# Block attention and a token mixer on one core: loading in float32 from the sync queue and casting on GpSimd, in place of casting in the GpSimd queue's transfers

## The chip, the core and the metric

The kernel runs on one core of a Trainium2 chip. A core has five engines that run side by side: TensorE (PE; its weight loads are listed apart as PEld), VectorE (DVE), ScalarE (ACT), GpSimd (POOL) and SyncE (SP). SP only issues transfers here; POOL issues transfers and can also compute. Sixteen DMA engines move the data between HBM and the on-chip memory SBUF. The metric is the device time of one execution in microseconds (us); less is better.

## What is computed

The inputs are q, k and v in float32, each 8 batches x 8 heads x 576 positions x 64, and three weights. First comes attention inside chunks of 64 positions (nine chunks a head), then a token mixer over the joined heads:

```python
scores = scale * np.matmul(q_c, k_c.transpose(0, 1, 2, 4, 3))   # per chunk of 64
attn = np.exp(scores); attn = attn / np.sum(attn, axis=-1, keepdims=True)
out = np.matmul(attn, v_c)
x = out.transpose(0, 2, 1, 3).reshape(B, S, H * D)              # 8 x 576 x 512
wq = x @ w_q; wk = x @ w_k                                       # 512 -> 64
W_tok = scale * np.einsum('bsd,btd->bst', wq, wk)
mixed = np.einsum('bst,btd->bsd', W_tok, x)
y = np.maximum(mixed, 0.0) @ w_out                              # 8 x 576 x 512, float32
```

## The kernel before, in words

The work is ordered by hand over batches; no scheduler moves anything, and each engine runs its instructions in the order of the text. Step n of the main loop runs the attention of batch n (`Attn`) woven with the mixer of batch n - 1 (`Mix`), and between them up to three pieces of the output product of an earlier batch (`fill`, `out_unit`). Step 8 has only the last mixer, and after it the remaining output pieces are flushed.

The attention of one batch has three groups g of q and k. `transposes(g)` (L150) turns q and k on PE into PSUM, and VectorE copies the result to SBUF (L156). `scores(g)` (L166) multiplies, ScalarE takes the exponential (L174). `av(hl)` (L193) multiplies with v, whose last column of ones also gives the row sums; VectorE takes the reciprocal (L201) and scales into `x_nat` (L202). The mixer transposes `x_nat` (`xt_part`, L226, copied by L233 and L235), projects it (`wqk`, L242), turns that (`wkn`, L254, copies L258 and L259), forms a 64 x 512 product (`gram`, L264) and applies it with the ReLU (`mixed`, L276 and L283). `out_unit` (L294) multiplies with w_out, ScalarE copies to `osb` (L302), and SP stores `osb` in four transfers (L307).

Loads are issued two batches ahead, by `load(b)`: `load_qk` (L100) and `load_v` (L113). All go out on POOL's queue, with float32 in HBM and float16 in SBUF, so the cast happens in the transfer. A q or k piece is 128 float32 (two rows of 64) for each partition and group, a v piece is one row of 64. For batch 0 q and k come in three parts each, for the others in one part for each half of the heads. SP issues only the stores.

The tile `in` of q and k has three buffers, as has v (`v_bufs`), so a load waits until the batch three before it has been used. `osb` has four buffers. PSUM is one pool of four buffers of two banks, shared by all products in turn. In `in` the half of the heads (hg) lies outside of the positions, so each transpose takes 64 columns for one hg and writes to 64 partitions: 24 of them in a group.

Of the kernel before, what the change touches and what calls it, by code (L numbers as in the profile page):

```python
# [9 lines left out]
F16 = mybir.dt.float16  # L10
F32 = mybir.dt.float32
# [5 lines left out]
def kernel(  # L17
# [15 lines left out]
    nc = tc.nc  # L33
    B, H, S, D = q.shape
    DM = moe_w_out.shape[0]
    DH = moe_w_q.shape[1]
    P = 128
    CH = 64
    NCH = S // CH
    NHG = 2  # L40
    NX = (H // NHG) * NCH
    NG = 3
    XG = NX // NG
    UG = XG // 4
# [6 lines left out]
    ts, ds = bass.ts, bass.ds  # L51

    const = ctx.enter_context(tc.tile_pool(name="const", bufs=1))
    in_pool = ctx.enter_context(tc.tile_pool(name="inp", bufs=3))
    qk_pool = ctx.enter_context(tc.tile_pool(name="qkp", bufs=2))
    e_pool = ctx.enter_context(tc.tile_pool(name="ep", bufs=2))
    rec_pool = ctx.enter_context(tc.tile_pool(name="rec", bufs=4))
# [7 lines left out]
    def psum(name, shape, dt=F32):  # L65
        return ps_pool.tile(shape, dt, name=name, tag="ps")

    ident = const.tile([P, P], F16, name="ident")
# [4 lines left out]
    NVB = 3  # L73
    v_bufs = [const.tile([P, NX, VP], F16, name=f"v{i}") for i in range(NVB)]
# [6 lines left out]
    for t in g_bufs:  # L81
# [3 lines left out]
    qr = [  # L85
        t.rearrange("b h s d -> b (h s d)")
        for t in (q, k)
    ]

    def load_qk(b):  # L90
        tiles = [
            in_pool.tile([P, NHG, NG * UG, P], F16, name=f"in{ti}", tag=f"in{ti}")
            for ti in range(2)
        ]
        parts = [ts(g, UG) for g in range(NG)] if b == 0 else [slice(0, NG * UG)]
        for part in parts:
            for ti in range(2):
                src = qr[ti][b].rearrange("(g u p e) -> g p u e", g=NHG, p=P, e=P)
                for hg in range(NHG):
                    nc.gpsimd.dma_start(  # L100
                        tiles[ti][:, hg, part, :], src[hg][:, part, :]
                    )
        return tiles

    def load_v(b):
        vt = v_bufs[b % NVB]
        src = v[b].rearrange("(g h) s d -> g (h s) d", g=NHG)
        src = src.rearrange("g (y o p r) d -> g o r p y d", o=2, p=32, r=2)
        dst = vt.rearrange("p (y o) d -> p o y d", o=2)
        for o in range(2):  # L110
            for half in range(2):
                for r in range(2):
                    nc.gpsimd.dma_start(  # L113
                        dst[ds(half * CH + r * 32, 32), o, :, 0:D],
                        src[(half + o) % 2, o, r],
                    )
        return vt

    wqk16 = const.tile([P, NDC, 2 * DH], F16, name="wqk16")
# [2 lines left out]
    def load_weights():  # L122
        nc.gpsimd.dma_start(
            wqk16[:, :, 0:DH], moe_w_q.rearrange("(i p) j -> p i j", p=P)
        )
        nc.gpsimd.dma_start(
            wqk16[:, :, DH:], moe_w_k.rearrange("(i p) j -> p i j", p=P)
        )
        nc.gpsimd.dma_start(wout16[:], moe_w_out.rearrange("(i p) m -> p i m", p=P))


    class Attn:
# [8 lines left out]
        def transposes(self, g):  # L141
            tp = psum("tp", [P, 2, 1024], F16)
            for ti in range(2):
                cols = tp[:, ti, 0 : UG * 2 * P].rearrange(
                    "p (u x r c) -> p u r x c", u=UG, r=2, x=4
                )
                for u in range(UG):
                    for r in range(2):
                        for hg in range(NHG):
                            nc.tensor.transpose(  # L150
                                cols[ds(hg * D, D), u, r],
                                self.qk_in[ti][:, hg, g * UG + u, ds(r * D, D)],
                                ident[:],
                            )
            sb = qk_pool.tile([P, 2, UG * 2 * P], F16, name="qk", tag=f"qk{g}")
            nc.vector.tensor_copy(sb[:], tp[:, :, 0 : UG * 2 * P])  # L156
            self.qk[g] = sb
# [131 lines left out]
    def out_unit(bp, rmx, t0, nt):  # L289

        op = psum("op", [P, 2, 512])
        for t in range(nt):
            for i in range(NDC):
                nc.tensor.matmul(  # L294
                    op[:, t, :],
                    lhsT=rmx[:, i, ts(t0 + t, P)],
                    rhs=wout16[:, i, :],
                    start=(i == 0),
                    stop=(i == NDC - 1),
                )  # L300
        osb = osb_pool.tile([P, 2, DM], F32, name="osb", tag="osb")
        nc.scalar.copy(osb[:, 0:nt, :], op[:, 0:nt, :])  # L302
        rows = out_rows[ds(2 * S * bp + P * t0, P * nt), :]
        rows = rows.rearrange("(t c p r) m -> c r p t m", c=2, r=2, p=32)
        for c in range(2):
            for r in range(2):
                nc.sync.dma_start(  # L307
                    rows[c, r], osb[ds(c * CH + r * 32, 32), 0:nt, :]
                )

    inputs = {}

    def load(b):
        inputs[b] = (load_qk(b), load_v(b))

    ctx.enter_context(tc.manual_schedule())

    load(0)
    load_weights()
    load(1)  # L320

    att, mix, outs = None, None, []

    def fill(n=1):
        for _ in range(n):
            if outs:
                outs.pop(0)()

    for n in range(B + 1):
        if n + 2 < B:  # L330
            load(n + 2)
        att = Attn(n) if n < B else None
        if att:
            att.transposes(0)
            att.transposes(1)
        if mix:
            mix.xt_part(0)
        if att:
            att.transposes(2)
        fill()  # L340
        if mix:
            mix.xt_part(1)
        if att:
            att.scores(0)
            att.scores(1)
        if mix:
            mix.wqk()
        fill()
        if att:
            att.scores(2)  # L350
            att.av(0)
            att.av(1)
        if mix:
            mix.wkn()
        fill()
        if mix:
            mix.gram()
        if att:
            att.av(2)
            att.av(3)  # L360
        if mix:
            for i in range(NDC):
                mix.mixed(i)
            bp, rmx = mix.b // 2, mix.rmx
            tiles = ((0, 2), (2, 2)) if mix.b % 2 == 0 else ((4, 2), (6, 2), (8, 1))
            outs += [
                lambda t0=t0, nt=nt, bp=bp, rmx=rmx: out_unit(bp, rmx, t0, nt)
                for t0, nt in tiles
            ]
        mix = Mix(n, att.x) if att else None  # L370
# [31 lines left out]
```

The softmax here doesn't subtract the row's maximum and nothing guards it: scores larger than these inputs give would overflow.

## Time and profile before

| what | value |
|---|---|
| time, median of 2 runs | 163.25 us (163.04 to 163.47) |
| the profiled execution's own time | 163.47 us |
| its span, from first to last instruction | 161.7 us |
| PE busy | 118.5 us (73%) |
| DVE, ACT busy | 64.9 us, 73.3 us |
| POOL busy (nearly all of it issuing transfers) | 82.1 us (51%) |
| read from HBM, written to HBM | 29.62 MB, 9.44 MB |
| loads of q and k of batches 1 to 7 | 288 KB each as written, 28 transfers |
| loads of v | 72 KB each as written, 64 transfers |
| stores | 128 KB x64 and 64 KB x16, 4.0 and 3.8 us from issue to landing |

How to read it: in a group of the profile stand the line, the engine, the operation, the tiles written and read, the count, then the busy time and the mean of one; after the bar the idle time just ahead of it and what ended it. In a timeline a row is the start, the busy time, the engine and line, with the idle time before it in brackets. "The stretches" are a view of chosen windows with the busy time of each engine (PE, PEld, DVE, ACT, POOL), then the clock granted to PE, the mean number of packets in work on each DMA engine, and GB/s written.

### The profile page before, as it was taken

The numbers are of one execution on the slowest core, as the hardware profiler recorded it, in microseconds if no ns is written. First come the engines' busy times: TensorE is split into PE (matmuls) and PEld (weight loads), VectorE is DVE, ScalarE is ACT, GpSimd is POOL, SyncE is SP. The second block draws the span as 40 slices with busy tenths as digits, with TensorE's granted clock in tenths as the row PEclk, the third lists the DMA queues.
The fourth block names the chain that finished last, engine by engine and source line by source line (L and its number), as shares of the span: only waits on it lengthen the run. The fifth ranks groups of instructions, "written<-read, shape, count | busy, mean of one in ns | idle before, by whom it ended". The sixth has DMA issues, their size and how long they took to land. (4 is left out here: it accounts for less than half of the span.)

```text
span 161.7 us, 5174 instructions
## 1 busy us (share of the span) xinstructions
PE 118.5 (73%) x2304; PEld 72.1 (45%) x2304; DVE 64.9 (40%) x119; ACT 73.3 (45%) x101; POOL 82.1 (51%) x113
## 2 busy tenths in 40 slices
PE   0567302494999589978994998789948997886840
PEld 0345201473475347635653565346535653442310
DVE  2032180166462556164616461646165516411000
ACT  3002300045366454756374637563747374844640
POOL 7999994597399397479349735961100000000000
PEclk9999999999599999999999699999999999999998
DMA  2999999999999999999999999999980044335165
GB/s 25 117 129 126 89 183 180 160 143 173 141 85 178 198 257 184 174 243 210 214 165 230 235 177 180 159 183 237 171 202 12 4 130 102 97 82 155 29 177 147
DMA packets 82886, 24.59 MB, mean 152 GB/s; under 512 B 77744, under 2 KB 78256, under 8 KB 82864
## 3 DMA queue, kind: packets, MB, share of 16 engines
q0 software_dynamic: 76976, 14.82, 110.9%
q1 hardware_dynamic: 5888, 9.44, 20.0%
q8 instruction: 18, 0.29, 0.7%
q14 instruction: 4, 0.03, 0.0%
HBM read 29.62 MB, written 9.44 MB: 242 GB/s over the span
## 5 line engine op out<-in xcount | busy, mean ns | idle before, releaser
L156 DVE COPY qk<-tp 128x1536 f16<-128x1536 f16 x24 | 22.4, 955 | 27.3 <-PE tp L150 27.3
L302 ACT COPY osb<-op 128x1024 f32<-128x1024 f32 (+1 forms) x20 | 18.4, 927 | 22.9 <-PE op L294 16.7
L202 DVE TENSOR_TENSOR x_nat<-xp,rec 128x640 f16<-128x640 f32 x32 | 26.4, 825 | 1.1
L174 ACT ACTIVATE est<-sp 128x768 f16<-128x768 f32 x24 | 18.7, 814 | 13.9 <-PE sp L166 13.9
L113 POOL DMA_DIRECT2D v_88<-in_v_dram x24 | 16.0, 685 | 14.5 <-DMA in_1885<-in_k_dram 5.0
L201 DVE RECIPROCAL rec<-xp 128x10 f32<-128x10 f32 x32 | 6.9, 215 | 38.0 <-PE xp L193 38.0
L113 POOL DMA_DIRECT2D v_87<-in_v_dram x24 | 15.9, 682 | 8.3 <-DMA in_1514<-in_k_dram 3.2
L233 ACT COPY xt<-tx 128x1152 f16<-128x1152 f16 x8 | 9.0, 1122 | 23.8 <-PE tx L226 23.8
L294 PE MATMUL op<-wout_104,rmx_102 128*128 128x512 f16 x72 | 17.4, 380 | 0.7 <-ACT rmx_102 L283 0.5
L294 PE MATMUL op<-wout_104,rmx_101 128*128 128x512 f16 x72 | 17.2, 379 | 0.5 <-ACT est L174 0.5
L264 PE MATMUL gp<-x_nat,wn 128*128 128x512 f16 x40 | 11.1, 412 | 7.9 <-DVE wn L259 7.9
L113 POOL DMA_DIRECT2D v_89<-in_v_dram x16 | 10.6, 687 | 8.5 <-DMA in_1131<-in_q_dram 2.7
L226 PE MATMUL tx<-ident,x_nat 128*128 128x128 f16 x160 | 12.1, 225 | 0.1
L226 PEld LDWEIGHTS <-x_nat 128*128 128x128 f16 x160 | 10.0, 101 | 2.8 <-issue 0.2
L235 DVE COPY xt<-tx 128x1152 f16<-128x1152 f16 x8 | 6.1, 756 | 11.6 <-PE tx L226 11.6
L193 PEld LDWEIGHTS <-est 64*64 64x64 f16 x640 | 7.6, 118 | 6.7 <-issue 3.8
L294 PEld LDWEIGHTS <-rmx_102 128*128 128x128 f16 x72 | 6.5, 98 | 8.5 <-ACT rmx_102 L283 1.9
L283 ACT ACTIVATE rmx_102<-mp 128x576 f16<-128x576 f32 x16 | 9.1, 656 | 2.3 <-PE mp L276 2.3
L283 ACT ACTIVATE rmx_101<-mp 128x576 f16<-128x576 f32 x16 | 9.1, 656 | 2.3 <-PE mp L276 2.3
L242 PE MATMUL wp<-xt,wqk_103 128*128 128x512 f16 (+1 forms) x64 | 9.5, 285 | 0.7 <-DVE xt L235 0.4
L294 PEld LDWEIGHTS <-rmx_101 128*128 128x128 f16 x72 | 6.4, 98 | 7.3 <-issue 0.8
L264 PEld LDWEIGHTS <-wn 128*128 128x128 f16 x40 | 3.4, 100 | 13.2 <-DVE wn L259 10.2
(85 smaller groups left out, 163.5 us busy)
## 6 DMA issues: line engine op xcount, KB each, us to landing
out_dram<-osb SPq DMA_DIRECT2D x64, 128.0 KB, 4.0
v_87<-in_v_dram POOLq DMA_DIRECT2D x24, 72.0 KB, 7.2
v_88<-in_v_dram POOLq DMA_DIRECT2D x24, 72.0 KB, 8.3
v_89<-in_v_dram POOLq DMA_DIRECT2D x16, 72.0 KB, 7.9
out_dram<-osb SPq DMA_DIRECT2D x16, 64.0 KB, 3.8
in_107<-in_q_dram POOLq DMA_DIRECT2D x6, 96.0 KB, 3.3
in_108<-in_k_dram POOLq DMA_DIRECT2D x6, 96.0 KB, 3.3
in_132<-in_q_dram POOLq DMA_DIRECT2D x2, 288.0 KB, 7.6
```

Of the source, the lines that this page charges most:

```text
L113: nc.gpsimd.dma_start(dst[ds(half * CH + r * 32, 32), o, :, 0:D], src[(half + o) % 2, o, r],)
L156: nc.vector.tensor_copy(sb[:], tp[:, :, 0 : UG * 2 * P])
L174: nc.scalar.activation(e.rearrange("p o y c -> p o (y c)"), sp[:, :, 0 : XG // 2 * CH], AF.Exp, scale=scale_attn,)
L193: nc.tensor.matmul(xs[o0 : o0 + CH, hg, j, 0 : D + 1], lhsT=self.e[g][r0 : r0 + CH, xl % 2, xl // 2, :], rhs=self.v[r0 : r0 + CH, x, 0 : D ...
L202: nc.vector.tensor_tensor(out=self.x.rearrange("p j (g h d) -> p g j h d", g=NHG, h=HH)[:, :, :, hl, :], in0=xs[:, :, :, 0:D], in1=rec[:, ...
L226: nc.tensor.transpose(tx[:, i2, ts(j, P)], self.x[:, j, ts(2 * half + i2, P)], ident[:],)
L233: nc.scalar.copy(xt[:], tx[:, :, 0:S])
L242: nc.tensor.matmul(wp[:, ds(c0, n)], lhsT=wqk16[:, i, :], rhs=self.xt[i // 2][:, i % 2, ds(c0, n)], start=(i == 0), stop=(i == NDC - 1),)
L264: nc.tensor.matmul(gp[:, 0:DM], lhsT=self.wn[:, j].rearrange("p t d -> p (t d)"), rhs=self.x[:, j, :], start=(j == 0), stop=(j == NJ - 1),)
L283: nc.scalar.activation(self.rmx[:, i, ds(self.col0, S)], mp[:, 0:S], AF.Relu, scale=scale_moe)
L294: nc.tensor.matmul(op[:, t, :], lhsT=rmx[:, i, ts(t0 + t, P)], rhs=wout16[:, i, :], start=(i == 0), stop=(i == NDC - 1),)
L302: nc.scalar.copy(osb[:, 0:nt, :], op[:, 0:nt, :])
```

## The change

The loads move to SP's queue and stay float32, into new tiles `raw0`, `raw1` and `rawv` with two buffers each. GpSimd then casts to float16: `cast_qk` makes six tiles a batch (q and k of each of the three groups, 768 elements for each partition) and `cast_v` one (2,304 elements). The casts of batch n + 1 are issued at the start of step n, after the loads of batch n + 2; the casts of batch 0 come before the loads of the weights, which stay on POOL. While it casts, `cast_qk` puts hg inside of the positions, so a transpose takes all 128 columns and both hg at once: 12 in a group. The stores stay on SP, in one order with the loads. In a step, the loads of batch n + 2 come before the step's stores.

```diff
+    raw_pool = ctx.enter_context(tc.tile_pool(name="rawp", bufs=2))
...
     def load_qk(b):
-        tiles = [
-            in_pool.tile([P, NHG, NG * UG, P], F16, name=f"in{ti}", tag=f"in{ti}")
+        src = [t[b].rearrange("(g u p e) -> g p u e", g=NHG, p=P, e=P) for t in qr]
+        raw = [
+            raw_pool.tile([P, NHG, NG * UG, P], F32, name=f"raw{ti}", tag=f"raw{ti}")
             for ti in range(2)
         ]
         parts = [ts(g, UG) for g in range(NG)] if b == 0 else [slice(0, NG * UG)]
         for part in parts:
             for ti in range(2):
-                src = qr[ti][b].rearrange("(g u p e) -> g p u e", g=NHG, p=P, e=P)
                 for hg in range(NHG):
-                    nc.gpsimd.dma_start(
-                        tiles[ti][:, hg, part, :], src[hg][:, part, :]
-                    )
-        return tiles
+                    nc.sync.dma_start(raw[ti][:, hg, part, :], src[ti][hg][:, part, :])
+        return raw
+
+    def cast_qk(raw, g):
+        pair = []
+        for ti in range(2):
+            t = in_pool.tile(
+                [P, UG, 2, NHG, D], F16, name=f"in{ti}{g}", tag=f"in{ti}{g}"
+            )
+            nc.gpsimd.tensor_copy(
+                t[:],
+                raw[ti][:, :, ts(g, UG), :].rearrange("p g u (r d) -> p u r g d", r=2),
+            )
+            pair.append(t)
+        return pair
 
     def load_v(b):
-        vt = v_bufs[b % NVB]
+        raw = raw_pool.tile([P, NX, D], F32, name="rawv", tag="rawv")
...
-                    nc.gpsimd.dma_start(
-                        dst[ds(half * CH + r * 32, 32), o, :, 0:D],
+                    nc.sync.dma_start(
+                        dst[ds(half * CH + r * 32, 32), o],
                         src[(half + o) % 2, o, r],
                     )
+        return raw
+
+    def cast_v(b, raw):
+        vt = v_bufs[b % NVB]
+        nc.gpsimd.tensor_copy(vt[:, :, 0:D], raw[:])
         return vt
...
                 for u in range(UG):
                     for r in range(2):
-                        for hg in range(NHG):
-                            nc.tensor.transpose(
-                                cols[ds(hg * D, D), u, r],
-                                self.qk_in[ti][:, hg, g * UG + u, ds(r * D, D)],
-                                ident[:],
-                            )
+                        nc.tensor.transpose(
+                            cols[:, u, r],
+                            self.qk_in[g][ti][:, u, r].rearrange("p g d -> p (g d)"),
+                            ident[:],
+                        )
...
     def load(b):
-        inputs[b] = (load_qk(b), load_v(b))
+        raws[b] = (load_qk(b), load_v(b))
+
+    def cast(b):
+        rqk, rv = raws.pop(b)
+        inputs[b] = ([cast_qk(rqk, g) for g in range(NG)], cast_v(b, rv))
...
     load(0)
+    cast(0)
     load_weights()
     load(1)
...
         if n + 2 < B:
             load(n + 2)
+        if n + 1 < B:
+            cast(n + 1)
```

More of the change, by code (lines that the diff above doesn't have):

```diff
@@ L97, in load_qk @@
             for ti in range(2):
-                src = qr[ti][b].rearrange("(g u p e) -> g p u e", g=NHG, p=P, e=P)
                 for hg in range(NHG):
-                    nc.gpsimd.dma_start(
-                        tiles[ti][:, hg, part, :], src[hg][:, part, :]
-                    )
-        return tiles
+                    nc.sync.dma_start(raw[ti][:, hg, part, :], src[ti][hg][:, part, :])
[12 more added lines that the diff above has]
+        return pair
     def load_v(b):
-        vt = v_bufs[b % NVB]
+        raw = raw_pool.tile([P, NX, D], F32, name="rawv", tag="rawv")
         src = v[b].rearrange("(g h) s d -> g (h s) d", g=NHG)
         src = src.rearrange("g (y o p r) d -> g o r p y d", o=2, p=32, r=2)
-        dst = vt.rearrange("p (y o) d -> p o y d", o=2)
+        dst = raw.rearrange("p (y o) d -> p o y d", o=2)
         for o in range(2):
@@ L311 @@
     inputs = {}
+    raws = {}
     def load(b):
-        inputs[b] = (load_qk(b), load_v(b))
+        raws[b] = (load_qk(b), load_v(b))
+    def cast(b):
+        rqk, rv = raws.pop(b)
+        inputs[b] = ([cast_qk(rqk, g) for g in range(NG)], cast_v(b, rv))
     ctx.enter_context(tc.manual_schedule())
     load(0)
+    cast(0)
     load_weights()
```

## The prediction

> **What bounds the kernel now.** I read the slices of the page first, then the tensor engine in order of time, then the list of waits, then the stretches.
>
> ```profile
> PE   0567302494999589978994998789948997886840
> DMA  2999999999999999999999999999980044335165
> PEclk9999999999599999999999699999999999999998
> ```
>
> One slice is 161.7 / 40 = 4.04 us. The DMA row is full from slice 1 to slice 28, that is to about 118 us, and PE is near full from slice 9 on. So two things look busy, and the order of time has to say which one sets the end.
>
> ```profile
> 19.12 1.31 PE L193 MATMUL xp<-v_87,est 64*64 64x65 f16 x78 [2.78 <-DMA v_87<-in_v_dram]
> ...
> 25.40 0.32 PE L150 MATMUL tp<-ident,in_132 128*64 128x128 f16 x1 [4.97 <-DMA in_132<-in_q_dram]
> 27.37 0.85 PE L150 MATMUL tp<-ident,in_132 128*64 128x128 f16 x11 [1.66 <-DMA in_132<-in_q_dram]
> 29.00 0.32 PE L150 MATMUL tp<-ident,in_133 128*64 128x128 f16 x1 [0.78 <-DMA in_133<-in_k_dram]
> 30.65 0.85 PE L150 MATMUL tp<-ident,in_133 128*64 128x128 f16 x11 [1.34 <-DMA in_133<-in_k_dram]
> ...
> 37.36 0.53 PE L193 MATMUL xp<-v_88,est 64*64 64x65 f16 x40
> ...
> 44.87 0.53 PE L150 MATMUL tp<-ident,in_146 128*64 128x128 f16 x12
> ...
> 60.43 0.53 PE L150 MATMUL tp<-ident,in_419 128*64 128x128 f16 x12
> ...
> 124.06 0.53 PE L150 MATMUL tp<-ident,in_1884 128*64 128x128 f16 x12
> ...
> 139.66 0.72 PE L226 MATMUL tx<-ident,x_nat 128*128 128x128 f16 x10
> ```
>
> The bracket names what ended the idle time. Up to batch 1 (in_132, in_133) every long bracket names a load. From batch 2 (44.87) on none does: batch 3 starts at 60.43, batch 7 at 124.06, the drain at 139.66. That is 94.8 us for six batches, 15.8 each (a clean one 15.6, one at a lower clock 16.3). The reader sees two regimes: 44.9 us of filling bound by loads, then 116.8 us (161.7 less 44.9) in which PE's own order is the limit.
>
> ```profile
> PE tp L150 <- DMA in_107<-in_q_dram: 6.7, 6, 4.3
> PE tp L150 <- DMA in_132<-in_q_dram: 6.6, 2, 5.0
> PE xp L193 <- DMA v_87<-in_v_dram: 2.8, 1, 2.8
> PE tp L150 <- DMA in_133<-in_k_dram: 2.1, 2, 1.3
> ```
>
> The list of waits agrees: the columns are total, times, longest, and only batches 0 and 1 appear. Last, two stretches in which nearly only one kind of load ran (q/k, then v):
>
> ```profile
> 26.50:29.00 2.50, 0.85 (x11) 0.60 (x12) 0.00 (x0) 0.00 (x0) 0.66 (x1) 1.00 1.83 182
> 29.60:32.00 2.40, 1.35 (x26) 1.35 (x28) 0.46 (x1) 0.00 (x0) 1.41 (x3) 1.00 2.37 153
> ```
>
> The last column is GB/s written as f16, so what is read as f32 is twice that: 364 and 306 GB/s. A batch has 2.36 MB of f32 q and k and 1.18 MB of v: 6.5 + 3.9 = 10.3 us. Yet the q loads of batches 2 to 7 follow each other by 12 to 15 us (31.54, 44.69, 56.80, 70.45, 84.54, 99.68 on POOL), because POOL's last v issues of each batch wait for earlier landings. A load stream that always has work could so be up to 3 us a batch faster than it is.
>
> **What the Trainium skill says.** "DMA: Bandwidth & Descriptors", SWDGE vs HWDGE vs iDMA: a cast in flight is possible from the GpSimd queue alone, and descriptors there are computed by GpSimd. The trace agrees on the second half: L113 is 64 issues of 0.66 to 0.74 us busy time on POOL. The same page, Issuing engines are not separate DMA queues: whoever issues, the same 16 engines do the work. So the move to SP gives no bandwidth of its own. "GPSIMD Engine Reference", 3.1: a one-input loop costs 1.03 to 1.8 cycles an element at 1.2 GHz, so an estimate of 0.66 to 1.15 us for 768 elements; no cast is in this trace, but two nearby rows are (below). "SBUF — State Buffer", Who interferes with whom: a VectorE instruction with at most one SBUF input outside the two-port modes does not block GpSimd. Here L156, L201, L202 and L235 all read PSUM (L202 with one small SBUF input), so I charge no contention; no run here shows it yet.
>
> **The change part by part.**
>
> Transposes. Before, 72 half transposes a batch: 44.87 to 46.34 for 48 and 47.00 to 47.79 for 24 give 2.26 us, 31 ns each, as two halves of the array run beside each other. After, 36 full ones. The nearest row is L226, ten full transposes from 46.34 to 47.00, 66 ns each: 36 x 66 = 2.37 us. Halving the count saves nothing; it costs 0.1 us a batch, 0.7 us over the six PE-bound ones. Bounds: 56 ns (two halves at the quickest pace, 12 in 0.33 us) to 73 ns (L226's busy time by ten), so -0.2 to +0.4 a batch.
>
> Issue. POOL loses 40 issues of q/k (0.76 to 1.04 us) and 64 of v (0.69), about 80 of its 82.1 us. SP gains these 104; its 80 stores took 0.43 us each (median), so 12 x 0.43 = 5.2 us a batch beside 10 stores' 4.3: under 15.6, hidden. In the start it matters: POOL needed until 16.07 us to issue batch 0; SP needs 20 x 0.43 = 8.6, and the stream fills.
>
> Casts. Six of 768 and one of 2304 elements a batch on POOL. A one-element memset took 99 ns, one of 128 elements 204 ns, a select over 128 elements 304 ns: 0.82 to 1.60 ns an element. So 0.73 to 1.33 us for a q or k cast, 1.99 to 3.79 for v; I take the middle, 1.03 and 2.9. A batch is 9.1 us (6.4 to 11.8), under 15.6, so hidden from batch 2 on. The casts run a batch or more ahead of PE: `in` and `v` have three buffers, and their waits on PE are for a batch three back. What is queued behind a waiting cast is the next cast, and at the start the three weight loads, needed only by L242 at 36 us.
>
> Loads. Same descriptors, f32 written instead of f16. I take the read rates above, 10.3 us a batch. The trace has no load without a cast. Bounds: below, 9.1 (an assumed 12% for the cast in flight, no row shows it); above, time going with bytes read plus written, x 1.33, 13.7 us.
>
> The filling, step by step. First landing: before, issue 1.29 to landing 4.30; SP starts at about 0.8, so q/k of batch 0 land by 2.8 + 6.5 = 9.3 and v by 13.2. v's cast ends at 16.1, where before v landed at 19.1. Then POOL issues the weights, 2.3 us. Batch 1's q and k land at 13.2 + 6.5 = 19.7; the weights' 1.6 MB share the engines, some 2.5 us, so 22.2, and v at 26. The casts then set the pace: k's first at 23.3, third at 27.5, v at 30.4. So the L193 of batch 1 starts at 30.5 instead of 37.36: 6.9 us earlier. If casts are at their upper bound, it is 32.7; at the lower, it is about 29.5, since PE's own order after k's landing then binds. Gain of the fill 4.7 to 7.9.
>
> After it, batch 2 starts at 44.9 - 6.9 = 38.0. With v of batch 1 at 26 and 10.3 a batch, k of batch 2 lands near 32.5, cast by 38, just in time; k of batch 3 near 43, with need at 53.6: hidden.
>
> Stores. They now stand behind loads in SP's order. The stores of batch 0's rows, ready near 44, wait until the load of batch 4 is issued, and that waits for batch 2's casts and for the eight loads before it. That load ends near 57, so they land near 60. Osb has four buffers, five units in two batches, so the fifth copy at about 60 can just be held: I charge 1.5 us once (0 to 5). The end is untouched: no loads stand before the last stores.
>
> Sum: 161.7 - 6.9 + 0.7 + 1.5 = 157.0 us of span; the profiled execution took 163.47, 1.8 more than its span, so 158.8. That execution is 0.2 over the median 163.25, so the forecast beside the median is 158.5 us, 2.9% faster.
>
> **Rivals.**
>
> *The gain is eaten.* The fill shortens by 3 us only, and L302's copies wait several times for osb. For it: the stores' late landing above, and ACT's copies already head PE's L254 waits (3.1 us). Against it: SP catches up once loads run ahead. 161.7 - 3 + 0.7 + 4, with 1.8 less 0.2: 165.
>
> *The single queue becomes the bound.* Loads and stores now share one in-order queue and the same engines. A batch stores 1.18 MB, at 364 GB/s 3.2 us. If loads take longer than 15.6 - 3.2 = 12.4 us a batch, PE waits for loads in every batch. At the upper bound 13.7 the period is 16.9, 1.3 more than PE's, over six batches 8 us, and the fill gains only 3: 161.7 - 3 + 8 + 0.7 + 1.6 = 169 us. For it: v's pieces of 256 bytes are small, and writes double. Against it: the stretches show 512-byte reads at 364 GB/s, and v's half-sized pieces went quicker per piece, so time followed bytes read. It decides from 12.4 us.
>
> *POOL becomes the bound.* At 2.25 ns an element 6912 elements are 15.6 us; at 2.4 it is 16.6 plus seven fixed costs of 0.1, 17.3. Eight batches are 138 us from about 3, the weights' issues 2.3, and from the last batch's first L193 (133.03) to the end are 28.7 more: 172 of span, 174 us. Against it: both nearby rows lie well under it.
>
> **How the numbers follow.** Forecast 0.52, gain eaten 0.19, queue 0.17, POOL 0.12. The likeliest's own range is 154 to 160.5. The range of 151 to 174 goes down to a fill at PE's limit with loads at 9.1 us and no held copy, and up past the queue's case; beyond it are half of POOL's case and a few per cent below. This kernel's measurement can tell about 2%. Faster by over 2% (under 160.0) 0.53, within 2% 0.19, slower 0.28.
>
> **What would show it.** Right: batch 2's first L150 near 38 us instead of 44.87, with POOL's cast rather than a DMA in its bracket; periods of 15.6 to 15.8 after it; casts near 1.03 and 2.9 us; L150 near 66 ns apart. Wrong: L150 or L193 waiting for casts in batches 4 to 7, either with POOL idle before them (the queue) or with POOL full (the casts); or L302 waiting for stores in most batches.

## The result, and the profile after

The kernel became slower: 191.61 us (190.65 to 192.57, two runs) where the kernel before took 163.25, a ratio of 1.174 (1.148 to 1.200). The forecast was 158.5 and the range ended at 174. Some executions of one kernel lie 1.5% and more above its fastest; the ratios with an interval below are those on record for the faster ones, so they can differ a little from the quotient of the medians. Of the profiled execution 190.1 us are span, 28.4 more than before.

The rows of 40 slices of the kernel after (one slice is 4.75 us):

```profile
PE   0552218727895998404995399739950599797760
...
PEclk9999999985999699965798559999996579999998
DMA  5999999999999999999999799999999834334445
```

The DMA row is full to slice 30, as it was before to slice 28 of a shorter span. What is new stands in the PE row: holes from slice 16 on (4 0 4, then 5 3, 3, and 5 0 5), where PE had been near full. Around most of them the clock row dips too, so PE also pays a little in its own pace: 122.2 us busy instead of 118.5.

PE in order of time (start, busy time, line, with the idle time before it and what ended it; the transposes are L166 now, the product with v is L209):

```profile
29.41 0.82 PE L166 MATMUL tp<-ident,in_181 128*128 128x128 f16 x6 [3.27 <-POOL in_181 L110]
...
40.84 0.51 PE L209 MATMUL xp<-v_91,est 64*64 64x65 f16 x40 [3.95 <-POOL v_91 L133]
...
48.75 0.49 PE L166 MATMUL tp<-ident,in_430 128*128 128x128 f16 x6
...
65.40 0.49 PE L166 MATMUL tp<-ident,in_749 128*128 128x128 f16 x6
...
88.04 2.10 PE L292 MATMUL mp<-wqkT_96,g_98 128*128 128x512 f16 x8 [9.37 <-ACT g_98 L287]
89.95 0.83 PE L166 MATMUL tp<-ident,in_1098 128*128 128x128 f16 x6
...
149.25 0.60 PE L209 MATMUL xp<-v_90,est 64*64 64x65 f16 x28 [6.57 <-ACT est L190]
...
168.10 0.72 PE L242 MATMUL tx<-ident,x_nat 128*128 128x128 f16 x10
```

Batch 2 starts at 48.75 (before 44.87, forecast 38.0). The drain starts at 168.10, so the six batches between take 119.35 us, 19.9 each, where they took 94.8. The rest, from the drain to the end, is 22.0 us in both. So the 28.4 us are 3.9 in the filling and 24.5 in the six batches.

Which wait ends last there? PE's own waits from 48.75 to 168.1 (total, times, longest):

```profile
PE mp L292 <- ACT g_98 L287: 12.8, 3, 9.4
PE xp L209 <- ACT est L190: 9.5, 2, 6.6
PE gp L280 <- DVE wn L275: 4.5, 6, 1.6
...
PE tp L166 <- POOL in_436 L110: 0.3, 1, 0.3
```

The first two lines are 22.3 of the 24.5 us. A reader in a hurry would put this down to ScalarE: no wait for a load, 0.3 us for a cast. ScalarE's own rows say otherwise. The first line is from its list of waits, the others from its order of time:

```profile
ACT osb L318 <- DMA out_dram<-osb: 34.7, 4, 11.3
```

```profile
86.92 0.59 ACT L318 COPY osb<-op 128x512 f32<-128x512 f32 x1 [11.34 <-DMA out_dram<-osb]
87.40 0.58 ACT L287 CAST g_98<-gp 64x512 f16<-64x512 f32 x1
```

The copy into `osb` waits 11.3 us for a buffer that an earlier store still reads, and the copy to `g` that PE needs is the next instruction in ScalarE's order. All four of these waits reach PE, as stalls of 9.4, 3.0, 3.2 and 6.6 us. The list of the kernel before has no wait of `osb` for a store. And why was the store late? SP's order of time (SPq is SP issuing transfers: start, busy time, what it issues, how many):

```profile
66.54 1.17 SPq L101 DMA_DIRECT2D raw_734<-in_q_dram  x2
67.81 4.14 SPq L101 DMA_DIRECT2D raw_735<-in_k_dram  x2
72.04 9.64 SPq L125 DMA_DIRECT2D rawv<-in_v_dram  x8
82.14 4.23 SPq L323 DMA_DIRECT2D out_dram<-osb  x8
86.47 1.26 SPq L101 DMA_DIRECT2D raw_1083<-in_q_dram  x2
```

SP hardly rests here: 1.2 + 4.1 + 9.6 = 15.0 us for the loads of one batch, 4.2 for eight stores, and the next batch's loads at 86.47, 19.9 us after the last. The two batches after that follow by 21.3 and 19.6 us; PE's mean period is 19.9. The stores at 82.14 stand behind 15 us of loads, whose issue takes as long as their transfer: 1.2 us for each v load, where a store in the kernel before took 0.43.

Last, stretches in which nearly only one kind of load ran (PE, PEld, DVE, ACT, POOL, clock, packets in work, GB/s written, which now equals GB/s read); first q and k, then v twice:

```profile
53.50:57.50 4.00, 3.96 (x76) 2.42 (x75) 0.76 (x1) 3.00 (x4) 2.11 (x1) 1.00 1.00 277
...
62.50:65.50 3.00, 3.00 (x51) 1.52 (x51) 2.00 (x4) 1.92 (x4) 2.00 (x3) 0.52 0.97 151
97.80:101.50 3.70, 2.66 (x79) 1.42 (x78) 1.18 (x3) 0.94 (x2) 3.58 (x5) 1.00 1.25 172
```

Before, q and k were read at 364 GB/s and v at 306. Now it is 277 to 299 (two further stretches gave 299) and 151 to 172. For a batch: 2.36 MB at 290 is 8.1 us, 1.18 MB at 160 is 7.4, together 15.5, in agreement with SP's 15.0. The prediction had 10.3.

So the reading to test was: the small pieces go slower when they arrive as float32, the loads and stores of a batch need about 20 us in one order, and the stalls on PE are how that shows.

### The profile page after: what moved, and what is told of

Same layout as the page of the kernel before. It is cut to its first block, busy times and chain, and to the rows that moved or that the text cites. A ratio compares the mean times of both kernels' runs of the same rounds, so it can differ in the third digit from the quotient of the medians.

```text
span 190.1 us, 4736 instructions
## 1 busy us (share of the span) xinstructions
PE 122.2 (64%) x2016; PEld 75.7 (40%) x2016; DVE 65.3 (34%) x119; ACT 72.6 (38%) x101; POOL 58.1 (31%) x65
## 5 line engine op out<-in xcount | busy, mean ns | idle before, releaser
L318 ACT COPY osb<-op 128x1024 f32<-128x1024 f32 (+1 forms) x20 | 18.4, 927 | 51.7 <-DMA out_dram<-osb 34.7
L209 PEld LDWEIGHTS <-est 64*64 64x64 f16 x640 | 8.3, 122 | 24.7 <-issue 14.9
L280 PE MATMUL gp<-x_nat,wn 128*128 128x512 f16 x40 | 12.5, 453 | 7.1 <-DVE wn L275 7.1
L292 PE MATMUL mp<-wqkT_96,g_98 128*128 128x512 f16 (+1 forms) x32 | 6.5, 354 | 12.9 <-ACT g_98 L287 12.8
L209 PE MATMUL xp<-v_90,est 64*64 64x65 f16 x240 | 4.0, 216 | 13.1 <-ACT est L190 6.6
L242 PEld LDWEIGHTS <-x_nat 128*128 128x128 f16 x160 | 11.0, 105 | 2.0 <-issue 0.2
L133 POOL CAST v_90<-rawv 128x2304 f16<-128x2304 f32 x3 | 6.3, 2109 | 12.4 <-DMA rawv<-in_v_dram 8.8
L133 POOL CAST v_91<-rawv 128x2304 f16<-128x2304 f32 x3 | 6.3, 2109 | 10.8 <-DMA rawv<-in_v_dram 6.2
```

What stands on the lines that cost most here:

```text
L133: nc.gpsimd.tensor_copy(vt[:, :, 0:D], raw[:])
L209: nc.tensor.matmul(xs[o0 : o0 + CH, hg, j, 0 : D + 1], lhsT=self.e[g][r0 : r0 + CH, xl % 2, xl // 2, :], rhs=self.v[r0 : r0 + CH, x, 0 : D ...
L242: nc.tensor.transpose(tx[:, i2, ts(j, P)], self.x[:, j, ts(2 * half + i2, P)], ident[:],)
L280: nc.tensor.matmul(gp[:, 0:DM], lhsT=self.wn[:, j].rearrange("p t d -> p (t d)"), rhs=self.x[:, j, :], start=(j == 0), stop=(j == NJ - 1),)
```

## The experiments

Each run was compared with the kernel before on the same chip; its median was 166.8 us there for e1, e2 and e3, 165.23 for x1, x2, x3 and f1, 165.45 for x4 and e5. The changed kernel itself was run only on the chip of its result, so a difference between its 1.174 and another run's ratio is good to some 3 or 4 percentage points. Where no interval stands, the runs gave none. The traces of the kernel before and after come from that chip too, on which the kernel before ran 1% faster (163.25) than on that of x1 to x4 and f1: batch starts compared across them can be off by 1 or 2 us.

### m1_queues: load rates by themselves, by queue and by piece size

Theory A: SP's queue is slow. Theory B: the small pieces are slow when written as float32. The kernel holds only loads, in stretches one after another, and stores zeros.

```diff
+    load_qk([sp], f32q)
+    load_qk([sp, act], f32q)
+    load_qk([pool], f32q)
+    long_qk([sp], f32q)
+    load_v([sp], f32v)
...
```

> No attention and no mixer: only loads, in stretches one after another, and zeros stored at the end. Two batches of q and k in float32 from SP; the same shared between SP and ACT; the same from POOL; the same bytes in pieces of 4.6 KB from SP; then v in float32 from SP, from SP and ACT, from POOL; then q and k, and v, cast in the transfer from POOL. In the changed kernel q and k came at about 280 to 299 GB/s and v at 151 to 172, with the DMA share at 1.0; before, with the cast, 364 and 306 GB/s read at a share of 1.8 to 2.4. Theory A (the queue: a queue of SP keeps one packet in work on each DMA engine, POOL's queue about two): SP alone 290 and 160 at share 1.0; POOL with float32 340 to 364 and about 300 at a share of 1.7 or more; SP with ACT as fast as POOL or nearly; the long pieces lose nothing from SP, above 340. Theory B (the type: writing float32 is what takes longer): POOL with float32 stays at 290 and 160 too, SP with ACT as well, and only the cast stretches reach 364 and 306. Theory C (SP issues too slowly): SP alone shows a share well under 1, and SP with ACT doubles it.

The stretches of it (DVE, POOL, clock, packets in work, GB/s), in the order: q/k from SP, from SP and ScalarE, from POOL without a cast, q/k from SP in pieces of 4.6 KB, v from SP.

```profile
4.00:17.00 13.00, 0.00 (x0) 0.00 (x0) 1.00 1.20 293
24.00:36.00 12.00, 0.00 (x0) 0.00 (x0) 1.00 1.20 291
44.00:56.00 12.00, 0.00 (x0) 3.81 (x4) 1.00 1.02 291
64.00:72.00 8.00, 0.00 (x0) 0.00 (x0) 1.00 1.02 417
76.00:84.00 8.00, 0.51 (x5) 0.00 (x0) 1.00 1.37 203
```

Theory A falls for q and k: 293, 291 and 291 GB/s, whoever issues (e2 below has v from POOL). This is what the Trainium skill says in "DMA: Bandwidth & Descriptors", Issuing engines are not separate DMA queues. Among these stretches the size of a piece decides: 417 GB/s in long pieces, 291 in 512 B, 203 in 256 B. The stretches with a cast at the end of this kernel ran beside its stores and are not used; m2 below has them.

### m2_order: does the mix of q, k and v, or the casts beside it, slow the loads?

Again only loads, three batches for each part: v alone, then q, k and v in the order of the changed kernel, then the same with POOL's casts beside, then cast in the transfer from POOL.

```diff
+    load_v([sp], f32v)
+    load_all([sp], f32q, f32v)
+    load_all([sp], f32q, f32v, cast=True)
+    load_all([pool], f16q, f16v)
```

> No attention and no mixer: only loads, three batches to a stretch, and zeros stored at the end. v alone in float32 from SP; then q, k and v batch by batch from SP, in the order of the changed kernel; the same with the casts on POOL following each batch; then the same order cast in the transfer from POOL. In the changed kernel v came at 151 to 172 GB/s, in a stretch of 16 v transfers alone at 203. If it is the order (v after q and k in one queue): 203 in the first stretch and about 160 in the second and third, 15 us a batch. If it is POOL's casts beside it: about 200 in the first two, 160 in the third. If neither: 200 in all three, 13.9 us a batch, and the rest of the changed kernel does it. The cast stretch: 10.3 to 11.5 us a batch.

Stretches, in pairs of q/k and v: from SP; from SP with casts on POOL beside; with the cast in the transfer (there GB/s read is twice what is shown):

```profile
25.00:27.00 2.00, 0.00 (x0) 0.00 (x0) 1.00 1.19 290
30.00:32.00 2.00, 0.00 (x0) 0.00 (x0) 1.00 1.37 206
66.00:69.00 3.00, 0.00 (x0) 2.37 (x3) 1.00 1.20 290
74.00:76.00 2.00, 0.00 (x0) 0.00 (x0) 1.00 1.24 203
116.00:119.00 3.00, 0.00 (x0) 3.00 (x6) 1.00 1.80 178
122.00:124.00 2.00, 0.00 (x0) 1.82 (x3) 1.00 2.40 152
```

Mixed order costs nothing (290 and 206 are the rates of each alone). With the cast in the transfer the same source pieces are read at 356 and 304 GB/s, the rates of the kernel before. Per piece on one of 16 engines: 512 B take 28.2 ns as float32 (512 x 16 / 290) and 23.0 with the cast; 256 B take 19.9 and 13.5. Two sizes give two terms: as float32 8.3 ns for every 256 B and 11.6 for the piece, with the cast 9.5 and 4.0. m1's long piece tests them: by the float32 terms its 18 times 256 B would take 161 ns, and 417 GB/s is 177, so the split holds to about 10%. By this estimate, what the cast in flight saves is mostly a fixed cost for each piece.

From the first issue of one batch to that of the next it took 14.0 us as float32, 14.8 with POOL's casts beside it, and 10.7 to 10.9 with the cast in the transfer. So the casts may explain a part of the way from 14.0 to the 15.0 to 15.5 of the full kernel; what else slows v there to 151 to 172 GB/s wasn't separated.

### x1_long_all and x2_long_v: the changed kernel with long pieces

The same bytes and the same transfers, but each partition reads one stretch of 4.6 KB; the numbers land in other places than the reference wants. x1 does it for v and, from batch 1 on, q and k; x2 for v alone.

```diff
-                    nc.sync.dma_start(raw[ti][:, hg, part, :], src[ti][hg][:, part, :])
+                    whole = qr[ti][b].rearrange("(g p e) -> g p e", g=NHG, p=P)
+                    nc.sync.dma_start(
+                        raw[ti][:, hg].rearrange("p u e -> p (u e)"), whole[hg]
+                    )
...
-                        src[(half + o) % 2, o, r],
+                        v[b].rearrange("h s d -> (h s d)").rearrange(
+                            "(n p e) -> n p e", n=8, p=32
+                        )[n],
```

> The changed kernel with the same bytes loaded in long pieces: from batch 1 on q and k, and in all batches v, go in runs of 4.6 KB for each partition in place of 512 and 256 bytes. Which row lands where is changed, so the output is not the reference's; counts and sizes of all instructions are the same. The stretches of loads alone gave 291 GB/s for float32 q and k in 512-byte pieces whichever queue issued them, 203 for v, and 417 for 4.6 KB pieces from SP. Theory B2 (small pieces written as float32 are what takes longer): a batch's loads fall from 15.3 us to 3.54 MB / 417 = 8.5, plus 3.8 of stores under PE's 15.6, so PE's order binds and the recorded forecast's case comes about: 156 to 161 us, ACT's waits for osb gone. Theory D (one order for loads and stores, or the casts' waits, whatever the rate): still 175 or more.

> The changed kernel with only v in runs of 4.6 KB (which row lands where is changed, so the output is not the reference's). Theory B2: v falls from 7.2 to 2.8 us a batch, so loads 10.9 and stores 3.8 to 4.7, about 15 us, just under PE's 15.6, with little room: 161 to 168. Theory D: 175 or more.

x1 has a ratio of 0.997 (0.992 to 1.001; the median of all its runs is 166.53 us): the loss of 17% is gone with the piece size alone. x2 took 177.37 and 181.28, 7 to 10% over the kernel before, so v makes up about half. Both missed their numbers (156 to 161, 161 to 168) on the slow side. The reason is in x1's list of waits (the line numbers are those of its own kernel; of the second line all but 0.9 us lies in the filling):

```profile
ACT osb L329 <- DMA out_dram<-osb: 14.3, 4, 5.6
...
PE tp L177 <- POOL in L116: 15.6, 11, 5.2
```

and in PE's order of time, where batch 2 starts 3.9 us before the 44.87 of the kernel before, though not the 6.9 of the forecast:

```profile
40.94 0.49 PE L177 MATMUL tp<-ident,in 128*128 128x128 f16 x6
```

From there the drain starts at 142.01, so the six batches take 101.1 us instead of 94.8. (This execution took 165.8 us; x1's runs lay between 163.0 and 169.6, so a part of these 6.3 us may be this execution's own.) Even with fast loads the stores stand behind them, ScalarE waits 14.3 us for buffers, and what the filling gains is lost again in the six batches.

### e3_osb8 and x4_long_osb8: eight buffers for osb, without and with long pieces

```diff
-    osb_pool = ctx.enter_context(tc.tile_pool(name="osb", bufs=4))
+    osb_pool = ctx.enter_context(tc.tile_pool(name="osb", bufs=8))
```

> The changed kernel with eight buffers of osb in place of four. Theory A: ACT's waits for osb go (34.7 us in four waits), but the queue's work stays: some 15.3 us of loads and 4.7 us of stores a batch in one order. The loads of batch 7 land where they did or up to 10 us earlier, so 180 to 190 us. Theory D (the copies' waits are the cost): the time falls by 25 us or more, to 165.

> Long pieces for q, k and v (which row lands where is changed, so the output is not the reference's) and eight buffers of osb. With long pieces alone the time equalled the kernel before: the second L150-like start of batch 2 came at 40.9 in place of 44.9, and ACT waited 14.3 us for osb. Theory S (after the pieces, the stores behind the loads' order eat the fill's gain): those waits go and the time falls by 4 to 7 us, 3 to 4% under the kernel before. If the waits only moved: within 1% of the kernel before.

e3: 184.73 us, ratio 1.103 (1.077 to 1.128). ScalarE waits for a store only once, 2.5 us, and the loss has moved to where it comes from:

```profile
POOL in L110 <- DMA raw<-in_k_dram: 33.9, 10, 6.0
POOL in L110 <- DMA raw<-in_q_dram: 30.9, 9, 8.0
...
PE tp L166 <- POOL in L110: 25.7, 18, 5.3
```

PE waits for casts, the casts for loads. Taking the waits for stores away was worth some 7 of the 17 percentage points; the stream of loads and stores itself sets the other 10.

x4: 160.34 us, ratio 0.969 (0.963 to 0.976), so 3.1% faster than before. ScalarE waits for no store. Batches 3 to 7 follow each other by 15.2 to 15.6 us, the six batches take 95.3 us (94.8 before), and batch 2 starts here:

```profile
42.07 0.49 PE L177 MATMUL tp<-ident,in 128*128 128x128 f16 x6
```

With long pieces and without the wait for stores the changed kernel runs at PE's own period and gains 3.1%, where 2.9% was forecast. That the two agree is in part luck: of the fill's 6.9 us only 2.8 are there, and these traces don't place the rest. The kernel before wasn't run with long pieces, so what they would give it isn't known.

### x3_quarter_stores, e1_stores_act, e5_stores_pool: where the stores stand

x3 keeps one store of four and leaves the rest of the output unwritten; e1 and e5 issue the stores from ScalarE or POOL.

```diff
-                nc.sync.dma_start(
+                if c == 0 and r == 0: nc.sync.dma_start(     # x3
+                nc.scalar.dma_start(                         # e1
+                nc.gpsimd.dma_start(                         # e5
```

> The changed kernel with one of every four stores kept and three left out, so most of the output is not written. Theory B2: the loads stay at 15.3 us a batch with 0.6 of gaps, the stores fall to about 1: some 16.5 a batch from the start, the last v cast near 130 and 29 more to the end, 160 to 168. Theory D: PE's order binds at once and the fill is 7 us shorter, 155 to 159. If the stores matter little: 180 or more.

> The changed kernel with its stores issued from ACT in place of SP; loads as they are. Theory A: stores no longer stand in the loads' queue, so the 34.7 us in which ACT's copies wait for osb go, and packets of the two queues are in work side by side. The loads alone take 15.3 us a batch and stay at or above PE's 15.6 with the 0.6 us of gaps, so about 168 to 173 us. Theory D (the order of stores behind loads is all that cost): PE's order binds again and the fill's gain shows, 160 or less. If neither the queue nor the order matters (theory B, DMA engines are just full): 185 or more.

> The changed kernel with its stores issued from POOL, after the casts of the next batch, so that SP has loads alone and the two have separate semaphores. Small float32 pieces as in the change. Theory B2 with S: loads 15.3 us a batch and up, stores beside them on the same engines but not ahead of them in the queue: 16 to 18 us a batch, 172 to 182 us, and ACT's waits for osb shorter than 34.7 us. If the shared queue was the main cost: 160 to 168.

x3: 177.19 us, ratio 1.077 (1.068 to 1.086), not the 160 to 168 expected. The few stores left still queue behind a batch of loads:

```profile
ACT osb L318 <- DMA out_dram<-osb: 21.3, 3, 10.0
```

Fewer bytes relieve the stream, but not the order.

e1: 229.8 us, ratio 1.371 (1.344 to 1.399). It should have parted stores from loads and did the opposite. SP's list of waits:

```profile
SPq L101 <- DMA out_dram<-osb: 69.2, 10, 7.9
```

The loads of q and k write no byte of `osb`, yet SP held them back 69.2 us for stores. In this trace the transfers of SP and ScalarE signal their landing on one set of eight semaphores (101 to 108), so a load that reuses a semaphore waits until the store that had it has landed. The run says nothing on the order of stores, which was its question.

e5: 182.2 us, ratio 1.101 (1.091 to 1.111), just past the slow edge of what was expected (172 to 182). Out of SP's order the stores wait behind POOL's casts; ScalarE's waits for them halve:

```profile
ACT osb L318 <- DMA out_dram<-osb: 18.0, 4, 8.0
```

Some 7 percentage points of the 17 come back, as with e3, by another way. No version that only moves or relieves the stores gets under 1.07.

### e2_loads_pool: float32 loads from POOL's queue

```diff
-                    nc.sync.dma_start(raw[ti][:, hg, part, :], src[ti][hg][:, part, :])
+                    nc.gpsimd.dma_start(raw[ti][:, hg, part, :], src[ti][hg][:, part, :])
...
-                    nc.sync.dma_start(
+                    nc.gpsimd.dma_start(
                         dst[ds(half * CH + r * 32, 32), o],
```

> The changed kernel with all loads issued from POOL, float32 to float32, casts on POOL as they are; stores on SP. Theory A: the loads come at the rates of before, 10 to 13 us a batch, but POOL now both issues (about 10 us a batch) and casts (7.0 us a batch), 17 us in one order with waits, so about 172 to 185, with v at 300 GB/s in its stretches. Theory B: v stays at 160 GB/s and the time at 190 or more.

225.89 us, outside theory A's 172 to 185 and in theory B's open range (190 or more). PE's first wait:

```profile
PE tp L166 <- POOL in L110: 76.1, 8, 34.9
```

POOL has to issue the loads of batch n + 2, and wait for landings to do so, before it can cast batch n + 1. So the time shows that order and not the rates. The rates are in its trace, and theory B had them right: from 39 to 43 us POOL loaded v alone, with no store and no cast beside it, at 165 GB/s; from 32 to 36 us it loaded q and k at 294. In float32 v is as slow from POOL as in the changed kernel (151 to 172), so SP's queue isn't what slows it.

### f1_first_on_sp: the kernel before with only the first batch's q and k on SP

The prediction held that the filling is bound by POOL's issue and the first loads. f1 keeps the cast in the transfer everywhere but in batch 0, whose q and k come as float32 from SP and are cast on ScalarE, idle then.

```diff
+        if b == 0:
...
+                        nc.sync.dma_start(
+                            raw[ti][:, hg, ts(g, UG), :], src[hg][:, ts(g, UG), :]
+                        )
...
+                    nc.scalar.copy(
+                        tiles[ti][:, :, ts(g, UG), :], raw[ti][:, :, ts(g, UG), :]
+                    )
```

> The kernel before, with only batch 0's q and k loaded as float32 from SP and cast on ACT, which idles there; all else stays with the cast in the transfer on POOL, which can now issue v of batch 0 from the first microsecond. The fill is 44.9 us before, bound by POOL's issue until 16 us and by loads until 31. Theory B2: 1 of 8 batches pays the slower pieces (2.36 MB at 290, 8 us, beside v at the same time), batches 0 and 1 and the weights (8.6 MB) land by about 29 in place of 35: 4 to 7 us faster than before on the same chip. If POOL's issue wasn't what held the fill: within 1%.

161.58 us, ratio 0.983 (0.977 to 0.989): 2.8 us, less than the 4 to 7 expected, and faster than both kernels. Batch 2 now starts at 41.80 instead of 44.87:

```profile
27.52 2.13 PE L167 MATMUL tp<-ident,in 128*64 128x128 f16 x35 [1.52 <-DMA in<-in_k_dram]
...
41.80 1.38 PE L167 MATMUL tp<-ident,in 128*64 128x128 f16 x42
```

Batch 1 still waits for its k, and batch 0 has become later: its scores begin at 18.50 us instead of 14.62, since PE waits for ScalarE's casts. What the fill could give was real but small.

## Why the prediction was wrong

**The step that failed** is "Loads", at "I take the read rates above, 10.3 us a batch". It carried rates that were read off transfers with a cast over to transfers without one. Its upper bound, 13.7 us, assumed that time could at most follow bytes read plus written. The lower bound took 12% off for the cast, the wrong sign. None of the three allowed that small pieces go faster with the cast than without it. Measured: 14.0 us alone, 15.0 to 15.5 in the kernel. Without the cast a 512 B piece takes 28.2 ns rather than 23.0, a 256 B piece 19.9 rather than 13.5 (m2), and from POOL's queue they are no faster (m1 for q and k, e2 for v). x1 settles that the load rate is the cause of the loss: with long pieces, read faster than the forecast had it, the loss is gone. The Trainium skill gives a reason to count pieces. "DMA: Bandwidth & Descriptors", Why small descriptors are slow, has a fixed three bus cycles for each packet, 11 instead of 8 for 256 bytes; an estimate from it is 27% of the time lost. m1 measured more: 203 against 417 GB/s, 51% lost. I had looked at bytes where that page counts pieces; on what a cast changes that section says nothing.

**"Stores: I charge 1.5 us once (0 to 5)"** was the second mis-sized term. It allowed one held copy; there were four, 34.7 us on ScalarE, and 22 us of it reached PE because `g` or `est` stood behind the copy. It depends on the first term, but not wholly: with fast loads there are still 14.3 us of such waits (x1), and with eight buffers the ratio falls from 0.997 to 0.969 (x4).

**The fill** was put at 38.0 for batch 2; it came at 48.75. Batch 0's v cast started at 20.00 instead of 13.2, and the first cast of batch 1's k ended at 29.35 instead of 23.3: the load step again. With long pieces, for q and k from batch 1 on, it came at 40.94 (x1), so of the 6.9 us gained by forecast 3.9 were there.

**The rival "The single queue becomes the bound"** named the right mechanism, with its decision point of 12.4 us a batch; the loads passed it. Its period, 16.9, was too short by 3.0 for the same reason: 13.7 + 3.2 was 15.0 + 4.2 plus rests. The sign that the prediction set for it, a wait for casts with POOL idle before, is what e3 shows. In the changed kernel itself the other sign appeared, waits for stores, so both names belong to one stream.

**What held.** Casts: 1.03 and 2.9 us forecast, 0.83 and 2.11 measured, 7.1 us a batch and hidden from batch 2 on:

```profile
69.68 2.11 POOL L133 CAST v_90<-rawv 128x2304 f16<-128x2304 f32 x1 [2.26 <-DMA rawv<-in_v_dram]
...
97.92 0.83 POOL L110 CAST in_1460<-raw_1084 128x768 f16<-128x768 f32 x1 [3.65 <-DMA raw_1084<-in_k_dram]
```

The 0.83 lies inside the 0.66 to 1.15 estimated from the Trainium skill, "GPSIMD Engine Reference", 3.1. So the rival with POOL as the bound had no part. No contention with VectorE: the scaling into `x_nat` takes 825 ns on the mean before and after, as the Trainium skill's "SBUF — State Buffer", Who interferes with whom, led me to charge. Transposes: a clean batch has 24 in 1.34 us and 12 in 0.67, counted from start to start, so 56 ns each, the lower bound rather than the 66 taken; 2.0 us a batch instead of 2.26, a small gain in place of a small loss. SP's issue at 0.43 us each was right for an empty queue only.

## What to carry to other kernels

In this case a load rate belonged to a piece size and to the types at both ends; when a cast leaves the transfer, measure the plain transfer by itself before the old rate is used again. When loads and stores share one order, ask how long a store can stand behind a batch of loads and how many buffers cover that, and read a stall on a compute engine back through its copy, its buffer and its store to the queue. A short stretch of loads with nothing beside it costs one run; m2's 14.0 us a batch stands past the 12.4 at which the prediction said that PE would wait for loads.

## What the runs showed of the hardware that was not expected

- A cast from float32 to float16 in the transfer made small pieces faster, not slower: 356 against 290 GB/s read in 512 B pieces, 304 against 206 in 256 B pieces. That the fixed cost of a piece falls from 11.6 to 4.0 ns is an estimate worked out from these; why it falls stays open. With the cast, 1.80 and 2.40 packets were in work on each DMA engine (m2), without it 1.19 and 1.37, so pieces overlapped more; whether that is the reason wasn't tested.
- Among the float32 stretches the number of packets in work doesn't give the rate: 1.20 and 1.02 went with the same 291 GB/s, 1.02 also with 417 (m1). Packets aren't alike either: the stretch from POOL shows 944 packets for the 3.49 MB that took 6,916 from SP and ScalarE.
- SP's issue of a transfer has no fixed length: 0.43 us for stores in the kernel before, 1.2 us for a v load in the kernel after, where the issues of a batch's loads (15.0 us) took as long as the transfers at the rates measured (15.5).
- Transfers issued by SP and ScalarE were not independent in e1, where they shared eight semaphores: loads waited 69.2 us for stores.
